# Layer 2 of a fused attention and two-layer MLP kernel: the second product from seven quarter products, in an order made by a list scheduler

## The chip, the cores and the metric

The kernel runs on one core of a Trainium2 chip. The metric is the device time of one execution in microseconds (us); the time before is the median of 3 runs. Engines: PE is TensorE's matmul stream and PEld its weight loads, DVE is VectorE, ACT is ScalarE, POOL is GpSimd, SP is SyncE, which issues most DMAs.

## The reference, cut to what matters

```python
attn = softmax(block_mask(q @ k.T / 8)) @ v     # 4 x 8 heads, 576 rows, 64 wide
x = attn.transpose(0, 2, 1, 3).reshape(2304, 512)
h = x @ w_in1;  g = where(h >= 1, h, where(h <= -1, 0, (h + 1) ** 2 / 4));  x = g @ w_out1
h = x @ w_in2;  g = h * cos(h);  out = g @ w_out2     # w_in 512 x 2048, w_out 2048 x 512
```

The change is in layer 2, the last line: `h = x @ w_in2`, `h * cos(h)`, and the product with `w_out2`.

## The kernel before, in words

All products on PE keep 32-bit accuracy by halves: an operand is split into a rounded part (hi) and the rest (lo), and each product is three matmuls, hi·hi, hi·lo, lo·hi. ACT makes the hi part, DVE the lo part (the helper `rest`, line 194).

Attention comes first, then layer 1 in five blocks of rows (four of 512 rows, and in the middle one of 256 rows, whose matmuls are therefore 256 columns wide), then layer 2 in `second()`. While layer 1 runs, `w_combine` fetches `w_in2` and `w_out2` in eight groups each, makes their parts on ACT, DVE and POOL, and stores them to DRAM: `w_in2` as seven combinations of its quarters, `w_out2` as it is.

Layer 2 takes the 2304 rows in three batches of 768. Each batch has two phases.

- First product (`first_product`, matmuls on line 900). Rows of x, features of x and columns of h are halved, so each of x, `w_in2` and h has four quarters, 11, 12, 21, 22. Seven products of sums of quarters (Strassen's scheme in Winograd's form) give all four quarters of h, where the plain product takes eight. A run is one of seven products (order `ROUND` = 1, 6, 2, 7, 5, 4, 3) for one of four column groups q: 12 matmuls of 384 columns. There are 28 runs. After a run, ACT copies its result out of PSUM or DVE adds it to a stored quarter. Run 3 goes on in the PSUM bank of run 5, two runs earlier, so its first matmul waits until DVE has read what run 5 left there. A tile of PSUM is two banks wide and there are four.
- `chain`: for each of 16 tiles of h, ACT makes the integer part of h/(2 pi) + 1/4, DVE takes it off in two steps (two constants, `C1` and `C2`), ACT takes the sine, DVE multiplies by h.
- Second product (`second_product`, line 985). It is the plain product: for each of 16 tiles, `pair` makes hi and lo, then two runs of 9 matmuls each, 512 columns wide, the tile as the weights and `w_out2` as the moving operand. 288 matmuls a batch, all into three PSUM tiles that are copied out at the end.

The weights come through a ring of ten buffers of 512 KB, fetched by SP up to nine ahead (`w2_fetch`, line 806). The next batch's x is loaded (`x2_load`, line 811) and split into seven operands (`x2_split`) in the second phase.

Engines run their instructions in program order. The order within `second()` comes from a clock of runs: `at(d, f)` puts f behind the run d steps later, and `chain` and `pair` start at most one tile each per run. `pin` (`keep_in_program_order`) fixes it.

Of the kernel before, what the change touches and what calls it, by code (L numbers as in the profile page):

```python
# [24 lines left out]
C1 = 6.28125  # L25
C2 = 2.0 * math.pi - C1

FLOOR = -0.5 + 2.0 ** -14


@with_exitstack
def attn_moe_moe_kernel(ctx: ExitStack, tc: tile.TileContext, q, k, v, w_in1, w_out1, w_in2, w_out2, out):
# [53 lines left out]
    wdi = [dram.tile([7, 128, 2, 512], F32, name=f"w2i{q}") for q in range(4)]  # L86
    wdo = [dram.tile([2, 128, 1024], F32, name=f"w2o{g}") for g in range(8)]
# [190 lines left out]
    def w_combine(g, which):  # L278
# [4 lines left out]
        plain = [M.F1.view((16 + 4 * i) * KB, [2, 512], F32R) for i in range(2)]  # L283
# [4 lines left out]

        def half_of(i):
            return v[:, 2 * i:2 * i + 2].rearrange("p a b -> p (a b)")  # L290

        def join(i):
            joined(half_of(i).bitcast(U32), raws[i])

        def hi(t, x):
            nc.scalar.activation(out=t, in_=x, func=ACTF.Copy)

        def lo(t, x, h):
            rest(t, x, h, nc.gpsimd)

        def split(d, t, x):
            if len(t.shape) == 4:
                h, l = t[:, :, 0], t[:, :, 1]
            else:
                h, l = t[:, 0], t[:, 1]
            at(d, lambda: hi(h, x))
            at(d + 1, lambda: lo(l, x, h))

        def combine():
            nc.vector.tensor_tensor(out=v[:, 3], in0=v[:, 2], in1=v[:, 3], op=ALU.add)  # L310
            sub(2, 0, 2)
            sub(0, 3, 0)
            sub(1, 1, 0)

        def store(i, n, t):
            dst = wdi[g // 2][i:i + n, :, g % 2].rearrange("i p x -> p i x")
            nc.gpsimd.dma_start(out=dst, in_=t.rearrange("p i a b -> p i (a b)").bitcast(F32))

        def store_plain(i):
            nc.gpsimd.dma_start(out=wdo[g][i], in_=plain[i].rearrange("p a b -> p (a b)").bitcast(F32))  # L320
# [5 lines left out]
        for i in range(2):  # L326
            at(1 + i, lambda i=i: join(i))
        at(3, free)
        if which == 1:
            for i in range(2):  # L330
                split(3 + i, plain[i], half_of(i))
                at(6 + i, lambda i=i: store_plain(i))
            return
        split(3, few[:, 0:2], v[:, 0:2])
        split(4, few[:, 2:3], v[:, 3:4])
        at(6, combine)
        for n in range(2):
            split(7 + n, many[:, 2 * n:2 * n + 2], v[:, 2 * n:2 * n + 2])
# [431 lines left out]
    HT = 384  # L770
    AT = {1: 0, 2: 1, 4: 2, 6: 3, 3: 4, 7: 5, 5: 6}
    ROUND = (1, 6, 2, 7, 5, 4, 3)
    NR = 10
# [4 lines left out]
    def l2_views():  # L778
        L2.runs, L2.loads, L2.slot = [], [], {}
        for b in range(NBK):  # L780
            for q in range(4):
                for i in ROUND:
                    L2.slot["a", b, q, i] = len(L2.loads)
                    L2.loads.append((wdi[q][AT[i]], (2, 512)))
                    L2.runs.append(("a", b, q, i))
            for q in range(4):
                for i in (2, 1):
                    for e in range(2):
                        for j in (1, 2):
                            L2.slot["b", b, q, 10 * i + j, e] = len(L2.loads)  # L790
                            L2.runs.append(("b", b, q, 10 * i + j, e))
                        L2.loads.append((wdo[2 * q + e][i - 1], None))
# [3 lines left out]
        L2.wo = [(42 + 4 * n) * KB for n in range(NR)]  # L796
# [3 lines left out]
    def w2_fetch(upto):  # L800
        while L2.fetched < min(upto, len(L2.loads)):
            src, dims = L2.loads[L2.fetched]
            t = M.A1.view(L2.wo[L2.fetched % NR], [1024], F32R).bitcast(F32)
            if dims:
                src = src.rearrange("p e n -> p (e n)")
            nc.sync.dma_start(out=t, in_=src)
            L2.fetched += 1
# [9 lines left out]
    def x2_split(pin=lambda i: i):  # L817

        X = {(r, c): L2.x[:, 2 * r:2 * r + 2, HT * c:HT * (c + 1)] for r in range(2) for c in range(2)}
        hi = lambda i, x: pin(nc.scalar.activation(out=L2.xq[i][:, :, 0], in_=x, func=ACTF.Copy))  # L820
        lo = lambda i, x: pin(rest(L2.xq[i][:, :, 1], x, L2.xq[i][:, :, 0]))
        sub = lambda o, a, b: pin(nc.vector.tensor_tensor(out=X[o], in0=X[a], in1=X[b], op=ALU.subtract))
        c11, c12, c21, c22 = (0, 0), (0, 1), (1, 0), (1, 1)

        def split(i, c):
            return [lambda: hi(i, X[c]), lambda: lo(i, X[c])]

        return (
            split(1, c11) + [lambda: sub(c11, c12, c11)] + split(3, c22) + [lambda: sub(c12, c22, c12)]
            + [lambda: sub(c22, c22, c11)] + split(6, c22) + split(2, c21) + [lambda: sub(c21, c22, c21)]  # L830
            + split(7, c12) + split(5, c11) + split(4, c21)
        )
# [18 lines left out]
    def l2_late():  # L851
# [10 lines left out]
        L2.u = Slots(M.F1, 6 * KB, 3 * KB, 2)  # L862
# [10 lines left out]
    def second():  # L873
# [18 lines left out]
        def first_product(run):  # L892
# [13 lines left out]
            if i in (1, 5):  # L906
                held[i] = at_, ps
# [269 lines left out]
```

## Time and profile before

| what | value |
|---|---|
| median of 3 runs | 972.42 us (972.08 to 972.62) |
| the profiled execution's own time | 972.27 us |
| its span, first to last instruction | 970.1 us |
| outside the span | 2.17 us |
| busy: PE, DVE, ACT, POOL | 955.4, 645.6, 495.0, 332.9 us |
| granted clock, share of full speed | 0.997 |

Busy times of one engine are the union of its instructions in time. For PE that says little about its pace, since matmuls overlap; the pace is read as time from one start to the next.

### The profile page before, as it was taken

How to read it: one execution, taken by the hardware profiler on the slowest of the kernel's cores; microseconds unless marked ns; L12 is line 12 of the kernel's file. 1: busy time of each engine (PE TensorE's matmuls, PEld its weight loads, DVE VectorE, ACT ScalarE, POOL GpSimd, SP SyncE). 2: the span in 40 equal slices, each digit the busy share in tenths (PEclk: the TensorE clock that was granted, in tenths of full speed). 3: DMA queues.
4: the chain of work that ended last, by engine and by line, in shares of the span. 5: the costliest groups of instructions: out<-in, count | busy, mean ns of one | idle time of the engine just before them, and what ended most of it. 6: DMA issues, size and time to landing. Idle time of an engine off the chain costs nothing.

```text
span 970.1 us, 15896 instructions
## 1 busy us (share of the span) xinstructions
PE 955.4 (98%) x5876; PEld 823.4 (85%) x5876; DVE 645.6 (67%) x1022; ACT 495.0 (51%) x1001; POOL 332.9 (34%) x421
## 2 busy tenths in 40 slices
PE   8999999999999999999999999999999999999997
PEld 7777888778888889988888889998889988899886
DVE  5778888777766686763647423688917889277870
ACT  5778888874454545453535222346513465134550
POOL 3567767766756574744552110000000000000000
PEclk9999999999999999999999999999999999999999
DMA  5755556345266557543352434883388744587411
GB/s 118 204 138 154 145 146 162 100 147 173 87 206 218 178 180 250 195 156 138 118 195 100 163 120 134 254 258 129 124 295 259 251 140 130 203 270 252 149 39 66
DMA packets 122509, 163.57 MB, mean 169 GB/s; under 512 B 62784, under 2 KB 91456, under 8 KB 122432
## 3 DMA queue, kind: packets, MB, share of 16 engines
q1 hardware_dynamic: 116288, 139.49, 46.2%
q0 software_dynamic: 6144, 23.07, 6.2%
q8 instruction: 47, 0.77, 0.4%
q14 instruction: 30, 0.25, 0.1%
HBM read 125.30 MB, written 37.22 MB: 168 GB/s over the span
## 4 chain that ended last, share of the span: by engine, by line
PE 79%; DVE 8%; ACT 8%; issue 2%; POOL 1%; DMA 1%; SPq 1%; ACTq 0%; DVEq 0%; POOLq 0%
PE q L985 20%; PE a L747 19%; PE h L701 19%; PE q L900 18%; ACT P L490 7%; DVE m L479 2%; DVE f L227 1%; DVE d L508 1%; DVE f L223 1%; DVE PT L560 1%; POOL m L194 1%; DMA rk<-in_k_dram 1%; PE s L451 1%; PE s L546 1%; PE s L577 1%
## 5 line engine op out<-in xcount | busy, mean ns | idle before, releaser
L985 PE MATMUL q<-m 128*128 128x512 f32 x864 | 196.4, 389 | 0.0
L985 PEld LDWEIGHTS q<-m 128*128 128x128 f32 x864 | 162.2, 188 | 33.5
L900 PE MATMUL q<-m 128*128 128x384 f32 x1008 | 175.3, 334 | 0.0
L900 PEld LDWEIGHTS q<-m 128*128 128x128 f32 x1008 | 174.9, 188 | 0.2
L747 PE MATMUL a<-g,m 128*128 128x512 f32 (+1 forms) x780 | 172.0, 368 | 0.4 <-DVE g L194 0.4
L747 PEld LDWEIGHTS a<-g,m 128*128 128x128 f32 x780 | 137.0, 189 | 25.1 <-DVE g L194 0.8
L194 DVE TENSOR_TENSOR g<-f,g 128x512 fp32r<-128x512 f32 (+1 forms) x80 | 78.4, 981 | 67.2 <-POOL g L191 66.9
L718 ACT ACTIVATE f<-h,half 128x512 f32<-128x512 f32 (+1 forms) x80 | 51.4, 642 | 132.6 <-PE h L701 120.3
L191 POOL TENSOR_SCALAR g<-f 128x512 fp32r<-128x512 f32 (+1 forms) x80 | 56.4, 704 | 162.6 <-DVE f L724 153.1
L519 POOL TENSOR_SCALAR P<-P,r 128x576 f32<-128x576 f32 (+2 forms) x144 | 91.2, 650 | 50.7 <-DVE r L511 31.3
L890 ACT ACTIVATE f<-f,hpi 128x768 f32<-128x768 f32 x48 | 45.1, 940 | 116.7 <-DVE f L887 116.6
L490 ACT ACTIVATE P<-s,m 128x288 f32<-128x288 f32 (+4 forms) x160 | 81.3, 523 | 36.3 <-DVE m L485 28.4
L701 PE MATMUL h<-m 128*128 128x512 f32 (+1 forms) x468 | 98.9, 360 | 0.0
L701 PEld LDWEIGHTS h<-m 128*128 128x128 f32 x468 | 79.1, 192 | 13.2 <-issue 0.7
L724 DVE SCALAR_TENSOR_TENSOR f<-f,h 128x512 f32<-128x512 f32 (+1 forms) x80 | 50.2, 627 | 43.7 <-ACT f L721 43.5
L701 PE MATMUL h<-x,m 128*128 128x512 f32 x312 | 75.9, 389 | 0.0
L223 DVE SCALAR_TENSOR_TENSOR f<-f 128x512 uint32<-128x512 uint32 x64 | 44.8, 721 | 38.8 <-ACT f L216 30.2
L479 DVE TENSOR_REDUCE m<-s 128x1 f32<-128x288 f32 (+4 forms) x160 | 67.1, 472 | 2.7 <-PE s L451 2.6
L701 PEld LDWEIGHTS h<-x,m 128*128 128x128 f32 x312 | 58.3, 188 | 11.8
L451 PE MATMUL s<-K,Q 128*128 128x288 f32 (+4 forms) x320 | 66.3, 462 | 1.3 <-ACT P L490 1.2
L887 DVE SCALAR_TENSOR_TENSOR f<-f 128x768 f32<-128x768 int32 x60 | 57.4, 957 | 4.7 <-ACT f L890 2.9
L577 PEld LDWEIGHTS s<-PT,rv 128*64 128x64 f32 x960 | 45.4, 137 | 14.1 <-ACT PT L562 9.3
(109 smaller groups left out, 1361.8 us busy)
## 6 DMA issues: line engine op xcount, KB each, us to landing
m<-w2i SPq DMA_DIRECT2D x84, 512.0 KB, 4.3
m<-w2o SPq DMA_DIRECT2D x48, 512.0 KB, 3.5
f<-in_moe_w_in_dram SPq DMA_DIRECT2D x32, 512.0 KB, 4.5
f<-in_moe_w_out_dram SPq DMA_DIRECT2D x32, 512.0 KB, 3.8
w2i<-f POOLq DMA_DIRECT2D x8, 1024.0 KB, 5.6
w2o<-f POOLq DMA_DIRECT2D x16, 512.0 KB, 3.1
w2i<-o POOLq DMA_DIRECT2D x8, 768.0 KB, 4.1
rk<-in_k_dram SPq DMA_DIRECT2D x32, 144.0 KB, 3.0
```

The costliest lines, as they stand in the source:

```text
L191: return nc.gpsimd.tensor_scalar(out=hi, in0=raw, scalar1=1.0, scalar2=1.0, op0=ALU.mult, op1=ALU.mult)
L194: return (eng or nc.vector).tensor_tensor(out=lo, in0=raw, in1=hi.bitcast(F32), op=ALU.subtract)
L451: mm = lambda o, l, r, **kw: pin(nc.tensor.matmul(out=o, lhsT=l, rhs=r, skip_group_check=True, **kw))
L479: i = P.top = nc.vector.tensor_reduce(out=m[:, c:c + 1], in_=o, axis=AX.X, op=ALU.max, negate=True)
L490: P.act = nc.scalar.activation(out=pr[:, a:b], in_=o, func=ACTF.Exp, bias=m[:, e:e + 1], accum_out=den[:, c:c + 1],)
L519: P.div = nc.gpsimd.tensor_scalar(out=pr[:, a:b], in0=pr[:, a:b], scalar1=r[:, e:e + 1], scalar2=1.0, op0=ALU.mult, op1=ALU.mult,)
L577: pin(nc.tensor.matmul(out=ps[64 * h:64 * h + 64, c0:c0 + nq], lhsT=V[:, j, h, :], rhs=PT[:, a:a + nq], start=(j == 0), stop=(j == i), ski ...
L701: nc.tensor.matmul(out=hps[s][:, 0:n_], lhsT=w[:, a, kk * 128:(kk + 1) * 128], rhs=x[:, b], start=(kk == 0 and n == 0), stop=(kk == NK - 1 ...
L747: nc.tensor.matmul(out=o, lhsT=w[:, a, dm:dm + 128], rhs=b, start=(f == 0 and n == 0 and c == 0), stop=(f == NF - 1 and n == 2), skip_grou ...
L887: pin(nc.vector.scalar_tensor_tensor(out=o, in0=a, scalar=c, in1=b, op0=ALU.mult, op1=ALU.add))
L900: pin(nc.tensor.matmul(out=ps[:, e, 0:HT], lhsT=w[:, e, a, 128 * kk:128 * (kk + 1)], rhs=L2.xq[i][:, kk, c], start=(not src and kk == 0 an ...
L985: pin(nc.tensor.matmul(out=ps[:, s], lhsT=t[:, e, a, 128 * m:128 * (m + 1)], rhs=w[:, o], start=(q == 0 and c > 20 and e == 0 and n == 0), ...
```

## The change

- `w_combine` treats both weights alike: `w_out2` too is combined to seven operands and stored as `w2o` in the shape of `w2i` (`AT` gives the places). ACT scales `w_in2` by 1/(2 pi) on the way (`turns`), so h comes out in turns.
- `cosine` replaces `chain`: in turns, the integer part comes off in one DVE instruction; the multiplication by 2 pi is in the last one.
- `second_product` is the seven-product scheme. A run is 18 matmuls of 256 columns, for one of seven products i and one of four groups q, in the order `ORDER`. The operands of products 5, 6, 7, 3 are differences or sums of tiles of g, made by `operand_sum` (two tiles in one instruction of 1536 elements). The results go out one product at a time, by ACT copies and DVE additions of 768 elements.
- All operations of `second()` are given to `Plan` with an engine, a cost and the data they read and write. `Plan.run` emits them: PE's runs stay in the order given, those of DVE, ACT and SP are taken as they come ready in its own reckoning, the one with the longest path behind it first.

```diff
+class Plan:
+    def add(self, eng, cost, reads, writes, fn):
...
+    def run(self):
...
+            i = min((i for i in ready[e] if ready_at[i] <= t), key=lambda i: (-left[i], i))
+            ready[e].remove(i)
+            self.ops[i][3]()
...
-    wdo = [dram.tile([2, 128, 1024], F32, name=f"w2o{g}") for g in range(8)]
+    wd = [[dram.tile([7, 128, 2, 512], F32, name=f"w2{'io'[which]}{q}") for q in range(4)] for which in range(2)]
...
+        def turns():
+            nc.scalar.activation(out=flat, in_=flat, func=ACTF.Copy, scale=INV2PI)
...
         def combine():
-            nc.vector.tensor_tensor(out=v[:, 3], in0=v[:, 2], in1=v[:, 3], op=ALU.add)
-            sub(2, 0, 2)
-            sub(0, 3, 0)
-            sub(1, 1, 0)
+            if which == 0:
+                nc.vector.tensor_tensor(out=v[:, 3], in0=v[:, 2], in1=v[:, 3], op=ALU.add)
+                sub(2, 0, 2)
+                sub(0, 3, 0)
+                sub(1, 1, 0)
+            else:
+                sub(0, 1, 0)
+                sub(1, 3, 1)
+                sub(3, 3, 0)
+                sub(2, 3, 2)
...
+    ORDER = [(q, i) for i in (1, 4) for q in range(3)] + [(3, 1), (3, 4)]
+    ORDER += [(q, i) for i in (2, 5, 6, 7, 3) for q in range(4)]
...
-            def s2():
-                stt(u, e, -C1, h)
-                stt(u, e, -C2, u)
...
+            act_(k, h, [G], [E], ACTF.Identity, bias=quarter)
+            tt(r, h, k, sub, [G, E], [E])
+            act_(r, r, [E], [E], ACTF.Sin, bias=hpi, scale=2.0 * math.pi)
+            do("V", 0.96, [E, G], [G], lambda: pin(nc.vector.scalar_tensor_tensor(
+                out=h, in0=h, scalar=2.0 * math.pi, in1=r, op0=ALU.mult, op1=ALU.mult
+            )))
...
+        FROM = {1: (11,), 2: (21,), 4: (22,), 5: (22, 12), 6: (22, 11), 7: (11, 12), 3: (21, 22)}
+        def operand_sum(i, q):
+            x, y = FROM[i]
+            tt(*(L2.g[o][:, 2 * q:2 * q + 4] for o in (x, x, y)), add if i == 5 else sub,
...
-            for m in range(3):
-                i, s = divmod(3 * j + m, 2)
...
-                for n, (a, o) in enumerate(((0, 0), (0, 1), (1, 0))):
-                    pin(nc.tensor.matmul(
-                        out=ps[:, s], lhsT=t[:, e, a, 128 * m:128 * (m + 1)], rhs=w[:, o],
...
+                for e in range(2):
+                    for m in range(3):
+                        for n, (a, o) in enumerate(((0, 0), (0, 1), (1, 0))):
+                            pin(nc.tensor.matmul(
+                                out=ps[:, m // 2, 256 * (m % 2):256 * (m % 2) + 256],
+                                lhsT=t[:, e, a, 128 * m:128 * (m + 1)], rhs=w[:, e, o],
...
+            do("P", 2.16, [T], [bk], emit)
...
+            if i in (1, 4, 5):
+                copy(i)
+            elif i == 2:
+                copy(0)
+                store(0, 0, 0)
+            elif i == 6:
+                plus(1, 1)
+            elif i == 7:
+                plus(0, 1)
+                tt(Y[4], Y[0], Y[4], sub, [("y", 0), ("y", 4)], [("y", 4)])
+                store(4, 1, 0)
+                tt(Y[5], Y[0], Y[5], add, [("y", 0), ("y", 5)], [("y", 5)])
+                store(5, 1, 1)
+            else:
+                plus(1, 1)
+                store(1, 0, 1)
```

Three places show what the order becomes. The first is PE at the start of the second product of the first batch, before the change (`q` with a number is a PSUM tile, `m` holds the operands):

```order
L985 MATMUL q_6711<-m 128x512 [waits DMAHW0_49,Activation_49]
L985 MATMUL q_6711<-m 128x512 x5
L985 MATMUL q_6718<-m 128x512 [waits PE_49]
L985 MATMUL q_6718<-m 128x512 x5
L985 MATMUL q_6729<-m 128x512 [waits DVE_49]
L985 MATMUL q_6729<-m 128x512 x5
```

Here two runs of 9 share one weight buffer and spread over three PSUM tiles. The same place on PE after the change:

```order
L1062 MATMUL q_6807<-m 128x256 [waits DMAHW0_49,Activation_49]
L1062 MATMUL q_6807<-m 128x256 x17
L1062 MATMUL q_6807<-m 128x256 [waits DMAHW1_49]
L1062 MATMUL q_6807<-m 128x256 x17
L1062 MATMUL q_6807<-m 128x256 [waits DMAHW2_49]
L1062 MATMUL q_6807<-m 128x256 x17
```

Each run of 18 now has a weight buffer and a pair of its own, stays in one PSUM tile, and its matmuls are half as wide.

The second place is DVE in the first batch's first product, column group q = 1, before the change. Rows of line 884 that read `q` are the additions after runs 7, 5, 4 and 3; line 887 takes the integer part off; the other row of 884 is the last step of a chain.

```order
L884 TENSOR_TENSOR g<-q_6411,w 128x768 [waits PE_49]
L884 TENSOR_TENSOR f<-q_6428,g 128x768 [waits DMASW3_49,DMASW4_49,DMASW2_49,DMASW5_49,DMASW1_49,DMASW6_49,DMASW0_49,DMASW7_49,DVE_49,PE_49]
L884 TENSOR_TENSOR g<-g,q_6444 128x768 [waits DVE_49,PE_49]
L884 TENSOR_TENSOR g<-g,f 128x768 [waits Activation_49]
L887 SCALAR_TENSOR_TENSOR f<-f,w 128x768 [waits Activation_49]
L887 SCALAR_TENSOR_TENSOR f<-f 128x768 [waits DVE_49]
L884 TENSOR_TENSOR w<-q_6428,w 128x768 [waits PE_49]
```

The additions after runs 7, 5 and 4 stand one behind the other. The same place on DVE after the change (988 has the additions, 935 takes the integer part off, 1025 is the last step of a chain, 251 makes a lo part):

```order
L988 TENSOR_TENSOR g<-q_6488,w 128x768 [waits DVE_49,PE_49]
L1025 SCALAR_TENSOR_TENSOR w<-w,f 128x768 [waits Activation_49]
L988 TENSOR_TENSOR f<-q_6506,g 128x768 [waits DMASW3_49,DMASW5_49,DMASW1_49,DMASW7_49,DVE_49,PE_49]
L935 TENSOR_TENSOR f<-w,f 128x768 [waits Activation_49]
L988 TENSOR_TENSOR g<-g,q_6524 128x768 [waits DVE_49,PE_49]
L935 TENSOR_TENSOR f<-f 128x768 [waits Activation_49]
L988 TENSOR_TENSOR w<-q_6506,w 128x768 [waits PE_49]
L1025 SCALAR_TENSOR_TENSOR w<-w,f 128x768 [waits Activation_49]
L1025 SCALAR_TENSOR_TENSOR f<-f 128x768 [waits Activation_49]
L251 TENSOR_TENSOR m<-f,m 128x2x384
```

A chain step that waits for ACT now stands between the additions after runs 7 and 5, another between those after 5 and 4, and a pair for the second product is made already here.

The third place is DVE late in the second product of the first batch, before the change (194 makes lo parts, of tiles `g`, `f`, `w` and of the next `x`; 822 is a difference of quarters of `x`).

```order
L822 TENSOR_TENSOR x<-x 128x2x384
L884 TENSOR_TENSOR g<-g,f 128x768
L194 TENSOR_TENSOR m<-g,m 128x2x384 [waits PE_49,Activation_49]
L194 TENSOR_TENSOR m<-x,m 128x2x384 [waits Activation_49]
L884 TENSOR_TENSOR w<-w,f 128x768
L194 TENSOR_TENSOR m<-f,m 128x2x384 [waits PE_49,Activation_49]
```

Chains still end here, between the lo parts. The same place on DVE after the change:

```order
L935 TENSOR_TENSOR f<-f,w 128x1536 [waits DVE_49]
L251 TENSOR_TENSOR m<-f,m 128x2x384 [waits PE_49,Activation_49]
L935 TENSOR_TENSOR w<-w 128x1536 [waits DVE_49]
L251 TENSOR_TENSOR m<-f,m 128x2x384 [waits PE_49,Activation_49]
L935 TENSOR_TENSOR f<-f,w 128x1536 [waits DVE_49]
L251 TENSOR_TENSOR m<-f,m 128x2x384 [waits PE_49,Activation_49]
```

The chains have moved ahead of this stretch, and operand sums of 1536 elements stand between the lo parts.

## Rows read from the trace of the kernel before

**Rows 1.** The page: busy us of each engine, share of the span, instructions.

```profile
PE 955.4 (98%) x5876; PEld 823.4 (85%) x5876; DVE 645.6 (67%) x1022; ACT 495.0 (51%) x1001; POOL 332.9 (34%) x421
```

**Rows 2.** The chain that ended last, layer 2: start us, us, what, matmuls.

```profile
594.09 58.26 PE q L900 x336
652.35 65.32 PE q L985 x288
717.67 58.26 PE q L900 x336
775.94 65.32 PE q L985 x288
841.26 58.26 PE q L900 x336
899.52 65.34 PE q L985 x288
```

**Rows 3.** The same chain in layer 1's block of 256 rows.

```profile
383.94 1.44 PE a L747 x12
385.38 1.44 PE h L701 x12
...
402.78 2.88 PE h L701 x24
```

**Rows 4.** Windows (us): busy of PE, PEld, DVE, ACT, POOL, granted clock, DMA share, GB/s.

```profile
380.00:400.00 20.00, 20.00 (x169) 20.00 (x169) 13.05 (x24) 10.85 (x23) 11.34 (x15) 1.00 0.52 187
400.00:500.00 100.00, 100.00 (x521) 86.17 (x520) 58.34 (x81) 45.32 (x80) 51.59 (x61) 1.00 0.40 143
```

**Rows 5.** Groups from 594 to 970 us, DVE.

```profile
L884 DVE TENSOR_TENSOR w<-w,f 128x768 f32<-128x768 f32 x24 | 22.8, 950 | 0.0
L884 DVE TENSOR_TENSOR f<-q,g 128x768 f32<-128x768 f32 x12 | 11.5, 958 | 1.2
L998 DVE COPY o<-q 128x1024 f32<-128x1024 f32 x3 | 3.7, 1225 | 44.9 <-PE q L985 44.9
```

**Rows 6.** Windows of layer 2's first four phases, columns as in rows 4.

```profile
593.90:652.20 58.30, 58.30 (x338) 58.27 (x337) 39.98 (x46) 24.15 (x29) 0.00 (x0) 1.00 0.82 257
652.20:717.60 65.40, 65.40 (x290) 54.15 (x290) 47.84 (x54) 30.39 (x37) 0.00 (x0) 1.00 0.48 161
717.60:776.00 58.40, 58.40 (x338) 58.37 (x337) 39.48 (x44) 23.52 (x28) 0.00 (x0) 1.00 0.81 270
776.00:841.00 65.00, 65.00 (x288) 53.82 (x287) 47.48 (x53) 30.39 (x37) 0.00 (x0) 1.00 0.42 137
```

**Rows 7.** Groups, ACT, from 594 to 970 us.

```profile
L890 ACT ACTIVATE m<-w 128x768 fp32r<-128x768 f32 x24 | 19.9, 830 | 0.5 <-DVE w L884 0.5
L890 ACT ACTIVATE o<-q 128x1024 f32<-128x1024 f32 x3 | 3.1, 1029 | 47.8 <-PE q L985 47.8
```

**Rows 8.** DMA issues from 594 to 970 us: KB each, median us to landing.

```profile
m<-w2i SPq DMA_DIRECT2D x74, 512.0 KB, 4.3
m<-w2o SPq DMA_DIRECT2D x48, 512.0 KB, 3.5
out_dram<-o SPq DMA_DIRECT2D x6, 512.0 KB, 2.8
x<-x2d SPq DMA_DIRECT2D x3, 512.0 KB, 6.3
out_dram<-x SPq DMA_DIRECT2D x3, 512.0 KB, 5.6
```

**Rows 9.** Line 900, its instructions: duration ns min/median/max, first and last start.

```profile
L900 PEldq EVENT_SEMAPHORE  x82: 51/51/51, 589.9 to 894.2; - x82
```

**Rows 10.** The timeline's end: start us, us, engine, line, what.

```profile
964.88 1.02 ACT L890 ACTIVATE x<-q 128x1024 f32<-128x1024 f32 x1 [1.69 <-PE q L985]
965.93 0.37 SPq L1002 DMA_DIRECT2D out_dram<-x  x1
```

**Rows 11.** Groups by line and shape, PE: busy us, mean ns of one, idle before.

```profile
L747 PE MATMUL a<-g,m 128*128 128x256 f32 x156 | 21.4, 283 | 0.0
```

More of the change, by code (lines that the diff above doesn't have):

```diff
@@ L778, in l2_views @@
     def l2_views():
-        L2.runs, L2.loads, L2.slot = [], [], {}
+        L2.runs = []
         for b in range(NBK):
[L781 to L792, printed above, removed]
+            L2.runs += [("a", b, q, i) for q in range(4) for i in ROUND]
+            L2.runs += [("b", b, q, i) for q, i in ORDER]
         M.X.renew(F32)
@@ L800, in w2_fetch @@
     def w2_fetch(upto):
[L801 to L806, printed above, removed]
+        while L2.fetched < min(upto, len(L2.runs)):
+            kind, b, q, i = L2.runs[L2.fetched]
+            which = "ab".index(kind)
+            nc.sync.dma_start(
+                out=L2.w[L2.fetched % NR].rearrange("p e a n -> p (e a n)").bitcast(F32),
+                in_=wd[which][q][AT[which][i]].rearrange("p e n -> p (e n)"),
+            )
             L2.fetched += 1
@@ new lines, in tt, with act_, taken @@
+        def tt(o, a, b, op, reads, writes, wide=1):
+            do("V", WIDE[wide], reads, writes, lambda: pin(nc.vector.tensor_tensor(out=o, in0=a, in1=b, op=op)))
+        def act_(o, a, reads, writes, func=ACTF.Copy, **kw):
+            do("A", 0.84 if func is ACTF.Copy else 0.93, reads, writes, lambda: pin(
+                nc.scalar.activation(out=o, in_=a, func=func, **kw)
+            ))
+        place = {r: n for n, r in enumerate(L2.runs)}
+        last, tiles = [-4, -3, -2, -1], {}
+        def taken(n):
+            at_ = min(range(4), key=lambda i: last[i])
+            tiles[at_, n] = None
+            last[at_] = 10 ** 9
+            return at_, n
@@ L1012, in second @@
[L1012 to L1025 removed]
+            key = held.pop(src) if src else taken(place[run])
@@ new lines, in first_product, with emit @@
+            bk = ("ps", key[0])
+            def emit():
+                w2_fetch(place[run] + NR - 1)
+                w, ps = L2.w[place[run] % NR], ps_of(key)
+                for e in range(2):
+                    for kk in range(2):
+                        for n, (a, c) in enumerate(((0, 0), (0, 1), (1, 0))):
+                            pin(nc.tensor.matmul(
+                                out=ps[:, e, 0:HT], lhsT=w[:, e, a, 128 * kk:128 * (kk + 1)], rhs=L2.xq[i][:, kk, c],
+                                start=(not src and kk == 0 and n == 0), stop=(kk == 1 and n == 2),
+                                skip_group_check=True,
+                            ))
@@ new lines, in second @@
+        next_x(1)
+        for b in range(NBK):
+            for run in L2.runs:
+                if run[1] != b or run[0] == "b":
+                    continue
+                first_product(run)
+                if run[2:] == (0, 1) and b + 1 < NBK:
+                    x_sums(b + 1)
+            if b + 1 < NBK:
+                x_splits(b + 1)
+            if b + 2 < NBK:
+                next_x(b + 2)
+            for q, i in ORDER:
+                if len(FROM[i]) == 2 and q % 2 == 0:
+                    operand_sum(i, q)
+                second_product(("b", b, q, i))
@@ L1028, in attn_moe_moe_kernel @@
+        plan.run()
     halves = [tuple(range(j, min(j + 2, NBLK))) for j in range(0, NBLK, 2)]
```

348 lines of the change are left out of this document (188 added, 160 removed).

## Prediction

> **What bounds the kernel now.** I read the page first: PE is busy 98% of the span, DVE 67%, ACT 51% [rows 1]. A busy PE need not be at its pace, so the second view is the chain that ended last. From 594.09 us to the last matmul it runs through PE alone, in six pieces: three first products of 58.26 us and three second products of 65.32 to 65.34 us [rows 2]. No other engine appears between them. The reader is to see that the 371 us of layer 2 are a count of matmuls times a pace: 58.26 us / 336 = 173.4 ns for 384 columns, 65.32 us / 288 = 226.8 ns for 512. So there are two questions: what the new matmuls take, and whether the other engines still keep up.
>
> **PE, the main term.** The second product is now 28 runs of 18 matmuls, 504 a batch and 1512 in all, in place of 864. They have 256 columns, and layer 1's block of 256 rows shows matmuls of that width, each with its own 128x128 weights, in the same order of parts (the same weights twice, then another): 12 in 1.44 us on either line, 24 in 2.88 us, so 120.0 ns [rows 3]. The window in the same stretch counts 169 in 20 us, 118 ns [rows 4]. I take 120.0.
>
> - Before: 65.32 + 65.32 + 65.34 = 195.98 us. After: 1512 x 0.120 = 181.44 us. Difference: **-14.5 us**.
> - The first products stay as they are: 3 x 58.26 us [rows 2].
>
> The Trainium skill prices this differently. Its page "TensorE: Matmul & The Clock Gate", section "Back-to-back issue gap", has a spacing of columns / 2.4 plus 2.5 ns, so 109.2 ns at 256 columns; by it the second product would take 165.1 us and the sum would be 941.8 us. The trace does not agree: it is 11 ns above that formula at 512 columns (226.8 against 215.8) and 11 ns at 256.
>
> **DVE.** A batch has, by the order, 20 additions after runs of the first product (as before), 32 chain steps where there were 48, 28 lo parts where there were 16, 5 additions on the way out where there was 1 copy, 11 operations for the next x (as before), and 8 operand sums of 1536 elements. That is 104 instructions where there were 96. One of 768 elements takes 0.95 us [rows 5], but they overlap at their ends: 46 fill 39.98 us, so 0.87 us of DVE's time each [rows 6]. A sum of 1536 elements has no row. It must lie between 1.225 us (1024 elements) and twice 0.950 us; by the slope between 950 and 1225 ns it is 0.95 + 768 x 0.275 / 256 = 1.78 us [rows 5], less the 0.08 us overlap 1.70 us. A batch then needs 96 x 0.87 + 8 x 1.70 = 97 us, and PE gives it 58.26 + 60.48 = 118.7 us: 82%, where it was 39.98 + 47.84 = 87.8 us of 123.6 [rows 6].
>
> The tightest stretch is the first batch's first product: from the first addition to the last the order has 57 DVE instructions, 49.6 us, and the additions can begin only two runs (4.2 us) after the phase does, so 54 us are left for them. Such a place costs nothing while PE's next run hides it. What can show is run 3: it goes on in the bank of run 5, with only run 4, 12 x 0.1734 = 2.08 us, between. The addition after run 5 takes 0.96 us [rows 5], so one DVE instruction (0.95 us) still fits ahead of it and two lose 0.96 + 2 x 0.95 - 2.08 = 0.78 us. The order has one ahead of it, a chain step that waits for ACT's sine. There are 12 such places: from 0 to 9.4 us. Before, this wait existed too, and PE idled 0.0 us in all of layer 2's chain [rows 2]; I stay near that row and take **+0.4 us**, half an instruction in all. Queued behind a late chain step on DVE are the addition, then run 3 on PE, and PE's order is fixed, so all that follows would move.
>
> **ACT.** A batch has 79 instructions. At 0.83 us for a copy of 768 elements, and less than the 1.03 us of 1024 for any other [rows 7], they take 66 to 81 us of 118.7; ACT matters as the one that the chain steps wait for.
>
> **Weights and SP.** Every run of the second product now fetches 512 KB: 28 a batch where there were 16. With the next x (1.57 MB) and the output (1.57 MB) a second product moves 14.7 + 3.1 = 17.8 MB in 60.5 us, 294 GB/s. First products moved 257 and 270 GB/s at a DMA share of 0.82 and 0.81 [rows 6]; by that ratio 294 GB/s is a share of 0.9. A fetch lands 3.5 to 4.3 us after issue, an x load 6.3 us [rows 8], and SP fetches nine runs ahead, 9 x 2.16 = 19 us. SP's queue holds the x loads and stores among the fetches, each waiting for DVE; 19 us covers such a wait. Cost 0; without that cover, see the rivals.
>
> **Waits on PE's queue.** A run that waits for more than one engine carries an extra semaphore instruction of 51 ns; the first products have 82 such and keep 173.4 ns [rows 2, 9]. At 120 ns there is less room beside it: from 0 to 84 x 0.051 = 4.3 us. I take 0, by the nearest row.
>
> **Layer 1.** Each of the eight groups of `w_out2` gets four DVE differences, two more hi and lo parts and larger stores, each group of `w_in2` an ACT scaling of 1024 elements, 1.03 us [rows 7]. In the stretch where `w_out2` is treated PE is busy 100.00 of 100 us while POOL is busy 51.59, DVE 58.34, ACT 45.32; and groups of `w_in2`, with about this work, passed while PE was busy 20.00 of 20 us [rows 4]. Cost 0; were ACT's part exposed, 8 x 1.03 = 8.2 us.
>
> **The end.** Before, ACT reads the last PSUM tile for 1.02 us, and the last store is issued at 965.93 us, 4.2 us before the span ends [rows 10]. Now DVE adds for 0.96 us and the store is 393 KB in pieces of 1 KB. By landing times of 2.8 to 6.3 us [rows 8] this is -1.4 to +2.1 us. I take 0.
>
> **Sum:** 972.27 (the profiled execution's own time, 0.15 us under the median) - 14.5 + 0.4 = **958.2 us**.
>
> **The rivals.**
>
> - *DVE late at run 3* (between 961 and 968 us). Two instructions ahead at all 12 places give 957.8 + 9.4 = 967.2 us, at half of them 962.5 us. For it: a step waiting for ACT stands at that place now, and the first stretch has DVE at nine tenths. Against: the 32 chain steps end early enough that the sum over a batch leaves DVE 22 us.
> - *DMA bounds the second product* (963 to 969 us). If 270 GB/s, the most that a phase showed, were all there is, 17.8 MB take 65.9 us, 5.4 us over, in the two batches that have a next x: 968.6 us. Against: the share was 0.81 then [rows 6].
> - *Slower: the weight loads bind at 256 columns.* The group of such matmuls is busy 21.4 us for 156, 137 ns each [rows 11], and in that stretch the weight loads are busy 20.00 of 20.00 us [rows 4], so any stumble of theirs shows. At 137 ns the 1512 take 207.1 us: 983.4 us. It decides from 195.98 / 1512 = 129.6 ns. Against: the chain's 120.0 ns, which spans whole pieces [rows 3]; the 21.4 us include overlapping ends. In the second product the weight loads were busy 54.15 of 65.4 us, 83% [rows 6]. The Trainium skill, "Perfetto Trace Analysis", section "Identifying the Most-Contended Engine", says to judge PE by the weight loads' busy share and not the matmuls'; by that rule the change takes the second product to its limit, which speaks against it, but the page names no loss.
> - *No gain.* Pairs made just in time: each run's third matmul waits for the lo part from DVE. 14.5 us / 84 runs = 0.17 us a run is enough to end at 972 us. Against: six pair buffers let DVE be six runs ahead.
> - *Faster: the fixed part of a matmul goes away.* From 384 to 512 columns the pace grows by 53.4 ns, 0.417 ns a column [rows 2], so 256 columns alone are 106.8 ns and some 13 ns a matmul are fixed. Were these hidden in the second product, it would take 1512 x 0.1068 = 161.5 us: 938.2 us. Against: 120.0 ns [rows 3] is 106.8 plus the same 13. The Trainium skill's spacing, above, points this way.
>
> **How the numbers follow.** My forecast 0.68 (956.5 to 961 us), DVE late 0.18, DMA 0.06, weight loads 0.04, no gain 0.03, no fixed part 0.01. The predicted time is that of the first. The range goes from 956 us (the end's gain of 1.4 us and no stall give 956.4) to 966 us, which takes in most of the second and a part of the third case, some 0.84. A measurement of this kernel tells about 0.2% (2 us) from no change. Faster: 0.68 + 0.18 + 0.06 + 0.01 = 0.93; same 0.03; slower 0.04.
>
> **What would show it.** In the chain, layer 2 is six pieces again, three of 58.3 us with 336 matmuls of 384 columns, three of 60.5 us with 504 of 256. PE's idle time before its groups stays under 1 us. DVE is busy about 82% of layer 2 and waits mostly for ACT. A time over 961 us should show PE waiting for DVE at runs 3 of the first product (line 970); DMA as the bound would show PE waiting for `w2o` fetches on line 1062; a pace over 125 ns on line 1062 without any wait would make the main term wrong.

## The result, and the profile after

The changed kernel takes 959.25 us (median of 4 runs, 958.83 to 959.64); the kernel before took 972.25 us beside it (971.69 to 972.62). The ratio is 0.9867, 95% interval 0.985 to 0.9884. 958.2 us were predicted. The profiled execution took 959.37 us, its span is 957.5 us (970.1 before) and the mean granted clock is 0.996.

The page of the changed kernel, busy us of each engine, beside [rows 1]:

```profile
PE 943.0 (98%) x6524; PEld 843.4 (88%) x6524; DVE 703.3 (73%) x1078; ACT 542.2 (57%) x1067; POOL 349.2 (36%) x437
```

PE is still busy 98%, with 648 more matmuls. As before, this row says nothing about the pace; the chain does. The chain that ended last, layer 2 of the changed kernel (start us, us, what, matmuls), beside [rows 2]:

```profile
596.48 58.26 PE q L970 x336
654.75 60.47 PE q L1062 x504
715.22 58.24 PE q L970 x336
773.46 60.47 PE q L1062 x504
833.93 58.24 PE q L970 x336
892.17 60.48 PE q L1062 x504
952.65 0.02 issue
952.67 0.96 DVE o L1089
```

The reader is to see three things. The six pieces are of PE alone, as before. A second product takes 60.47 us where it took 65.32 us, and 60.47 us / 504 = 120.0 ns a matmul. And layer 2 begins at 596.48 us, 2.39 us later than before, which no step of the prediction had.

The account, from the two profiled executions: layer 2 to its last matmul 356.17 us for 370.77 us (-14.6); its start +2.4; from the last matmul to the end of the span 4.85 us for 5.24 us (-0.4); outside the span 1.87 us for 2.17 us (-0.3). The sum is -12.9 us, which is 959.37 - 972.27.

Windows of the changed kernel's first four phases (columns as in [rows 4]), beside [rows 6]:

```profile
596.40:654.70 58.30, 58.30 (x338) 58.30 (x337) 49.66 (x56) 38.81 (x47) 0.00 (x0) 1.00 0.76 259
654.70:715.20 60.50, 60.50 (x506) 60.50 (x505) 51.59 (x52) 27.87 (x35) 0.00 (x0) 1.00 0.79 269
715.20:773.40 58.20, 58.20 (x338) 58.20 (x337) 48.43 (x54) 36.33 (x44) 0.00 (x0) 1.00 0.80 280
773.40:833.90 60.50, 60.50 (x506) 60.50 (x505) 48.63 (x49) 28.71 (x36) 0.00 (x0) 1.00 0.76 258
```

DVE (third number) has gone from 39.98 to 49.66 us in the first product and from 47.84 to 51.59 us in the second; over layer 2's six phases it is busy 288.38 of 356.2 us, 81%. The weight loads (second) are now busy in every microsecond of the second product. The DMA share is 0.76 to 0.80 and PE waits for no fetch. The granted clock is 1.00.

In layer 2 PE's waits are empty. In layer 1 there is this one, of the waits of PE (us in total, times, longest):

```profile
PE a L801 <- DVE g L251: 1.3, 3, 0.8
```

1.0 us of it falls between 400 and 500 us. The window there, beside the last of [rows 4]:

```profile
400.00:500.00 100.00, 99.03 (x515) 84.73 (x514) 77.14 (x104) 49.47 (x90) 66.00 (x73) 1.00 0.53 189
```

PE was busy 100.00 us here and is now busy 99.03 us; DVE went from 58.34 to 77.14 us and POOL from 51.59 to 66.00. In this stretch `w_out2` gets its parts.

### The profile page after: what moved, and what is told of

It reads as the page before. It is cut to its first block, busy times and chain, and to the rows that moved or that the text cites. A ratio compares the mean times of both kernels' runs of the same rounds, so it can differ in the third digit from the quotient of the medians.

```text
span 957.5 us, 17583 instructions
## 1 busy us (share of the span) xinstructions
PE 943.0 (98%) x6524; PEld 843.4 (88%) x6524; DVE 703.3 (73%) x1078; ACT 542.2 (57%) x1067; POOL 349.2 (36%) x437
## 4 chain that ended last, share of the span: by engine, by line
PE 76%; DVE 10%; ACT 8%; issue 2%; POOL 2%; DMA 1%; SPq 0%; ACTq 0%; DVEq 0%; POOLq 0%
PE q L1062 19%; PE a L801 18%; PE q L970 18%; PE h L755 18%; ACT P L544 7%; DVE m L533 2%; DVE f L284 1%; DVE d L562 1%; DVE f L280 1%; DVE PT L614 1%; POOL m L251 1%; DVE g L251 1%; PE s L505 1%; DVE f L343 1%; PE h L166 1%
## 5 line engine op out<-in xcount | busy, mean ns | idle before, releaser
L1062 PE MATMUL q<-m 128*128 128x256 f32 x1512 | 181.9, 283 | 0.0
L1062 PEld LDWEIGHTS q<-m 128*128 128x128 f32 x1512 | 181.8, 192 | 0.0
L970 PEld LDWEIGHTS q<-m 128*128 128x128 f32 x1008 | 174.7, 188 | 0.1
L251 DVE TENSOR_TENSOR g<-f,g 128x512 fp32r<-128x512 f32 (+1 forms) x80 | 70.8, 885 | 54.8 <-POOL g L248 54.7
L631 PE MATMUL s<-PT,rv 128*64 128x128 f32 (+1 forms) x960 | 52.4, 260 | 2.3 <-ACT PT L616 2.3
```

Source lines behind the costliest of these rows:

```text
L251: return (eng or nc.vector).tensor_tensor(out=lo, in0=raw, in1=hi.bitcast(F32), op=ALU.subtract)
L631: pin(nc.tensor.matmul(out=ps[64 * h:64 * h + 64, c0:c0 + nq], lhsT=V[:, j, h, :], rhs=PT[:, a:a + nq], start=(j == 0), stop=(j == i), ski ...
L970: pin(nc.tensor.matmul(out=ps[:, e, 0:HT], lhsT=w[:, e, a, 128 * kk:128 * (kk + 1)], rhs=L2.xq[i][:, kk, c], start=(not src and kk == 0 an ...
L1062: pin(nc.tensor.matmul(out=ps[:, m // 2, 256 * (m % 2):256 * (m % 2) + 256], lhsT=t[:, e, a, 128 * m:128 * (m + 1)], rhs=w[:, e, o], start ...
```

## The experiments

Each run stands beside runs of the kernel before on the same chip; these took 972.45 us in the runs of layer 1 and of half width, 974.5 us in those of DVE, order and ring, and 972.99 us in the last four. Absolute times are compared within one of these groups, and otherwise ratios. The first three runs ask where the 2.4 us at the start of layer 2 come from.

**1. Without w_out2's differences.** This kernel leaves out the four differences of each group of `w_out2`. Parts and stores are issued as in the changed kernel, on data that isn't combined.

```diff
             else:
-                sub(0, 1, 0)
-                sub(1, 3, 1)
-                sub(3, 3, 0)
-                sub(2, 3, 2)
+                return
```

> The changed kernel, with the combination of w_out2 left out: its four DVE differences a group and what follows them (parts of the four combined operands and their store), so the output is not the reference's. In the changed kernel layer 2 starts at 596.48 us, 2.4 us later than before, 1.9 us of it lost between 415 and 430 us, where w_out2 is prepared beside layer 1. Theory (the added preparation holds the lo parts of layer 1's g on DVE): without it the loss goes, layer 2 starts at 594.1 to 595.1 us, PE's wait for DVE on line 801 falls from 1.3 us to under 0.5, and the time is 957.0 to 958.0 us. Rival (the loss is the chance of one execution, or comes from the larger stores of the first three operands, which stay): 596 to 597 us again and 959.2 us.

Measured: 957.45 us (956.99 to 957.9), ratio 0.9845, interval 0.983 to 0.986. The expectation speaks of what follows the differences as left out too; it was not, so this is the cost of the four differences alone. Window of this run:

```profile
400.00:500.00 100.00, 100.00 (x520) 86.16 (x520) 57.37 (x82) 48.64 (x89) 66.07 (x74) 1.00 0.55 194
```

PE is back at 100.00 of 100 us, with POOL as busy as in the changed kernel. So DVE's 32 differences cost PE time in layer 1. In the changed kernel the chain that ended last leaves PE there and runs through a difference (line 343) and a lo part of `g` (line 251):

```profile
408.53 2.09 DVE f L343
...
423.54 0.96 DVE g L251
424.49 1.44 DVE f L343
428.00 2.46 DVE g L251
```

In the kernel before and in this run, the same stretch of the chain is of PE alone.

**2. w_out2's lo parts on DVE in place of POOL.** This gives DVE more work and POOL less.

```diff
-            rest(t[:, :, 1], x, t[:, :, 0], nc.gpsimd)
+            rest(t[:, :, 1], x, t[:, :, 0], nc.gpsimd if which == 0 else nc.vector)
```

> The changed kernel, with the lo parts of w_out2 made on DVE and not on POOL. Theory A (stretching: DVE's two-tensor operations take 0.78 us where 0.42 us is their undisturbed time, while POOL makes lo parts beside them; POOL's work is what stretches them): w_out2's DVE differences of 256 elements fall from 775 ns to under 550 ns, the loss goes, layer 2 starts at 594.1 to 595.3 us, time 957.0 to 958.3 us. Theory B (queueing: what stands ahead of the lo parts of g on DVE is too much, however fast): DVE has 32 more instructions in this stretch, the loss grows, layer 2 starts at 597 us or later, time 959.5 us or more.

Measured: 957.88 us (957.28 to 958.11), ratio 0.9849, interval 0.9834 to 0.9863. Groups of DVE in 400 to 530 us (busy us, mean ns of one, idle before), of the changed kernel:

```profile
L343 DVE TENSOR_TENSOR f<-f 128x256 f32<-128x256 f32 x32 | 24.8, 775 | 3.5 <-POOL o L251 3.2
L251 DVE TENSOR_TENSOR g<-f,g 128x512 fp32r<-128x512 f32 x20 | 21.7, 1087 | 15.4 <-POOL g L248 15.4
L778 DVE SCALAR_TENSOR_TENSOR f<-f,h 128x512 f32<-128x512 f32 x20 | 13.6, 681 | 2.4 <-ACT f L775 2.4
```

and of this run:

```profile
L251 DVE TENSOR_TENSOR g<-f,g 128x512 fp32r<-128x512 f32 x20 | 14.9, 747 | 4.8 <-POOL g L248 4.8
L343 DVE TENSOR_TENSOR f<-f 128x256 f32<-128x256 f32 x32 | 14.8, 462 | 0.0
L251 DVE TENSOR_TENSOR f<-f 128x512 fp32r<-128x512 f32 x16 | 14.5, 908 | 0.5
L778 DVE SCALAR_TENSOR_TENSOR f<-f,h 128x512 f32<-128x512 f32 x21 | 14.3, 681 | 3.6 <-ACT f L775 3.5
```

The same 32 differences take 462 ns each where they took 775, and the lo parts of `g`, for which PE waits, 747 ns where they took 1087. In 400 to 500 us DVE has 131 instructions for 104, and yet is busy 78.80 us for 77.14. POOL's lo parts, running beside them, had stretched DVE's subtractions. The stretching itself is not new: in the kernel before, POOL's lo parts of `w_out2` ran beside layer 1 too, and the lo parts of `g` took nearly as long, as they still do in run 1 (its row is the second):

```profile
L194 DVE TENSOR_TENSOR g<-f,g 128x512 fp32r<-128x512 f32 x21 | 20.7, 986 | 22.2 <-POOL g L191 22.1
L251 DVE TENSOR_TENSOR g<-f,g 128x512 fp32r<-128x512 f32 x20 | 18.7, 934 | 33.9 <-POOL g L248 33.9
```

PE lost nothing in either. The starts and durations in the changed kernel's trace show which of POOL's work matters. Of DVE's 28 subtractions of 512 elements on line 251 between 400 and 530 us, the 12 with nothing of POOL beside them took 677 to 695 ns, the 5 beside POOL's roundings alone 880 to 1120 ns, and the 11 beside its subtractions 692 to 2445 ns. Run 2 leaves the roundings on POOL, so 747 ns is still above the undisturbed time.

**3. The four differences on POOL.**

```diff
-        sub = lambda o, a, b: nc.vector.tensor_tensor(out=v[:, o], in0=v[:, a], in1=v[:, b], op=ALU.subtract)
+        eng = nc.gpsimd if which == 1 else nc.vector
+        sub = lambda o, a, b: eng.tensor_tensor(out=v[:, o], in0=v[:, a], in1=v[:, b], op=ALU.subtract)
```

> The changed kernel, with the four differences of each group of w_out2 on POOL and not on DVE. Theory B (queueing on DVE): DVE's queue is as before the change, the loss goes, layer 2 starts at 594.1 to 595.3 us, 957.0 to 958.3 us. Theory A (stretching by POOL's work): POOL gets 32 more two-tensor operations of about 0.75 us, so its rounding of g comes later and DVE's lo parts of g are stretched as much or more: layer 2 starts at 596.5 us or later, 959.3 to 963 us.

Measured: 958.39 us (956.96 to 958.79), ratio 0.9852, interval 0.9837 to 0.9867. The lo parts of `g` on DVE stay long, and those of 256 elements have become longer (925 ns in the changed kernel):

```profile
L251 DVE TENSOR_TENSOR g<-f,g 128x512 fp32r<-128x512 f32 x20 | 21.7, 1085 | 39.8 <-POOL g L248 39.8
L251 DVE TENSOR_TENSOR g<-f,g 128x256 fp32r<-128x256 f32 x8 | 10.4, 1306 | 2.9 <-POOL g L248 2.9
```

The whole time lies between the ranges of the two theories. DVE has fewer instructions here, and PE still waits for it, once, for 0.5 us. Long lo parts with a short queue cost nothing in run 1, and a long queue of short subtractions cost nothing in run 2. So both matter: how much stands in DVE's queue, and how long each subtraction takes beside POOL's work.

Whole times of these runs differ by little more than their intervals. One stretch can be read more closely: from the 480th matmul of layer 1's first product (line 755, 701 before) to layer 2's first matmul, worked out from the starts in each trace. What lies ahead of it, attention above all, is not in it: over all the profiled executions the stretch begins anywhere between 390.4 and 392.9 us.

| kernel | us | gaps between PE's starts of more than 0.26 us |
|---|---|---|
| before | 202.95 | none |
| changed | 204.83 | 0.47, 0.29, 1.15, 0.34 us, from 407 to 431 us |
| changed, once more (below) | 204.83 | 0.47, 0.28, 1.14, 0.34 us, the same places |
| 1, no differences | 202.95 | none |
| 2, lo parts on DVE | 203.06 | none |
| 2, once more (below) | 203.01 | none |
| 3, differences on POOL | 203.74 | 0.82 us, at 412 us |

So of the 2.4 us, 1.9 us are the change's; the other 0.5 us stand ahead of the stretch and are within its varying start. The loss repeats: runs 5 to 10, whose layer 1 is the changed kernel's, have 204.37 to 204.82 us, so it is 1.4 to 1.9 us, and run 4, with the layer 1 of before, has 202.95 us. Of the 1.9 us the four gaps hold 1.3 us over the pace of 0.227 us; the rest is spread too thin to name. The gaps stand beside the first two of the eight groups of `w_out2`, whose differences begin at 405 and 424 us, in or just behind the block of 256 rows, which PE leaves at 426 us. The six later groups, with the same work, show no gap. What sets the first two apart was not tested.

**4. The kernel before at half width.** Each matmul of the plain second product is made as two of 256 columns. It tells the change of width from the change of scheme.

```diff
-                for n, (a, o) in enumerate(((0, 0), (0, 1), (1, 0))):
-                    pin(nc.tensor.matmul(
-                        out=ps[:, s], lhsT=t[:, e, a, 128 * m:128 * (m + 1)], rhs=w[:, o],
+                for x in range(2):
+                    for n, (a, o) in enumerate(((0, 0), (0, 1), (1, 0))):
+                        pin(nc.tensor.matmul(
+                            out=ps[:, s, 256 * x:256 * (x + 1)], lhsT=t[:, e, a, 128 * m:128 * (m + 1)],
+                            rhs=w[:, o, 256 * x:256 * (x + 1)],
```

> The kernel before, with each matmul of the second product cut into two of 256 columns: the same columns, twice the matmuls (1728). Theory (a matmul takes 13.2 ns plus 0.417 ns a column, whatever its width here, and weight loads at every matmul add nothing): the second product takes 1728 x 0.120 = 207.4 us, 11.4 us more, 983.7 us in all; the chain shows 576 matmuls in 69.1 us. Rival (at 256 columns the weight loads are the limit only in long streams, or the first trace's 137 ns busy a matmul was the truth): 1728 x 0.137 = 236.7 us, 1013 us. Rival (no fixed part): 972 us.

Measured: 984.99 us (984.51 to 985.48), ratio 1.013, interval 1.0113 to 1.0147. Its chain:

```profile
653.37 69.11 PE q L986 x576
...
780.73 69.11 PE q L986 x576
908.08 69.12 PE q L986 x576
```

69.11 us / 576 = 120.0 ns again, whatever the scheme. The three pieces are 11.4 us longer than in [rows 2], and another 1.0 us of the 12.5 us is the later start of layer 2, 595.11 us. The change's gain is thus two effects: an eighth less of multiplication, 24.5 us of 195.98, less 10 us for narrower matmuls, since 120.0 ns is 6.6 ns more than half of 226.8 and 1512 x 6.6 ns = 10 us.

**5. A third DVE step in every chain.** An operation that changes nothing (the maximum of a tensor with itself), 16 a batch.

```diff
             tt(r, h, k, sub, [G, E], [E])
+            tt(r, r, r, ALU.max, [E], [E])
```

> The changed kernel with a third DVE step in each chain, as before the change (a maximum of the remainder with itself, in place of the second constant): 48 more DVE instructions of 0.87 us, 42 us, so DVE is busy about 94% of layer 2 in place of 82%. Theory (DVE's slack is real and the order is made anew around the extra step, so PE waits at a few runs 3 only): 0 to 3 us more, 959.2 to 962.5 us. Rival (at 94% an engine whose steps alternate with ACT's cannot keep up): PE waits 5 us or more for DVE in layer 2, 964 to 980 us.

Measured: 986.91 us (982.32 to 988.23), ratio 1.0113, interval 1.0086 to 1.0139; span 980.4 us. My theory fell. The rival's waits of 5 us or more came, and the time lies above its range too. PE's waits of the profiled execution, the fastest of the four:

```profile
PE q L1063 <- ACT m L939: 14.6, 3, 6.1
PE q L1063 <- DVE m L251: 2.4, 3, 1.2
```

All stand at one place, between the 108th and the 112th matmul of each second product. 108 / 18 is six runs, so it is the seventh, (q = 3, i = 1): the first that needs the last tile of quarter 11, whose chain ends late. Windows of PE around it in the second batch (busy of PE, granted clock, DMA share, GB/s):

```profile
778.00:786.00 8.00, 8.00 (x68) 1.00 0.85 263
786.00:794.00 8.00, 5.24 (x44) 0.99 0.77 253
794.00:802.00 8.00, 3.71 (x15) 0.50 0.02 6
802.00:810.00 8.00, 8.00 (x62) 0.87 0.54 181
810.00:818.00 8.00, 8.00 (x69) 1.00 0.76 235
```

A wait costs twice: PE idles, and in the window in which it begins again the granted clock is 0.50, the level of 1.2 GHz; it is back at 1.00 in the last window. 48 steps of 0.87 us are 42 us of DVE's time; layer 2 with the end (594.96 to 980.4 us) became 24.4 us longer than in the changed kernel, 17.0 us of it these waits.

**6. Without the list scheduler's order.** The operations are emitted as they are listed.

```diff
+        for op in self.ops:
+            op[3]()
+        return
```

> The changed kernel without the list scheduler's order: all operations of layer 2 are emitted as they are listed, each chain right behind its addition, each pair right ahead of its run, the seven splits of the next x ahead of the second product. DVE then waits for ACT twice in every chain with the next addition behind it: 4 chains of 2 x 0.95 + 2 x 0.93 us and 5 additions of 0.95 us a column group are 20 us where PE needs 14.6, so 21 us a first product, and some 6 us at the start of two second products. Theory: 1020 to 1045 us. Rival (in-order queues and six pair buffers even it out, so the order matters little): under 970 us.

Measured: 1191.51 us (1190.78 to 1193.22), ratio 1.2222, interval 1.2204 to 1.224; far over what I expected. PE's waits and a window of the first batch:

```profile
PE q L1065 <- ACT m L942: 90.3, 21, 16.1
PE q L973 <- ACT f L988: 61.2, 9, 6.8
PE q L1065 <- DVE m L254: 10.0, 21, 1.3
```

```profile
597.00:700.00 103.00, 65.76 (x327) 0.80 0.47 150
```

The scheme is the same, and in these rows PE waits 161.5 us, for pairs (`m`) and for copies of PSUM by ACT (line 988 of this run's kernel). The mean granted clock of the span is 0.919. On this chip the changed kernel would take 0.9867 x 974.5 = 961.5 us, by estimate, so the order is worth 230 us against this listing. It says nothing of the kernel before, which had an order of its own, from its clock of runs.

**7. The addition after run 5 three times**, in the first product. It tests the rival on run 3 by force.

```diff
-                out_(22, add, 21)
+                for _ in range(3):
+                    out_(22, add, 21)
```

> The changed kernel with the addition after each run 5 done three times (the same result each time), so that the last of them ends late; the order has one or two other DVE instructions among them. Theory (run 3 must wait for it and only run 4, 2.08 us, hides it): 4 or 5 instructions of 0.87 to 0.95 us are 3.5 to 4.6 us, 1.4 to 2.5 us of PE idle at each of 12 places, 17 to 30 us: 976 to 989 us, with PE waiting for DVE on line 970. Rival (PE is ahead of need there and DVE's slack of a fifth takes it): under 963 us.

Measured: 999.41 us (998.87 to 999.95), ratio 1.0249, interval 1.0229 to 1.027. PE's waits:

```profile
PE q L970 <- DVE f L988: 28.6, 12, 3.3
```

12 waits at the 12 places that the prediction named, 28.6 us, within what the expectation had for waits. The time is above the expectation. A window of PE behind the third wait of the first batch and the piece of the chain there show why:

```profile
640.00:650.00 10.00, 6.66 (x31) 0.84 0.48 148
```

```profile
645.47 16.44 PE q L970 x84
```

The granted clock is 0.84, and 16.44 us / 84 = 196 ns a matmul, where 173.4 ns is the pace at the full clock. I had priced the wait and not the clock behind it: from layer 2's first matmul to the end of the span this run takes 402.1 us for 361.0 us, 41.1 us more, of which the waits are 28.6 us.

**8. A ring of five buffers**, SP four fetches ahead and not nine.

```diff
-    NR = 10
+    NR = 5
```

> The changed kernel with five weight buffers in place of ten, so that fetches go four runs ahead (8.3 to 8.6 us) and not nine. Theory (a fetch lands 3.6 to 4.2 us after its issue and the DMA share of 0.8 leaves room): no loss in the steady run, 958.5 to 960.5 us. Rival (the DMAs are near their limit, and x loads and stores of 3.1 MB a batch need the deep ring as a store): PE waits for fetches on lines 970 and 1062 when x is loaded or results go out, 2 us or more: 961 to 970 us.

Measured: 961.57 us (960.17 to 965.92), ratio 0.9875, interval 0.9846 to 0.9904. The ratio can't be told from the changed kernel's. In the profiled execution (960.38 us) PE's starts show one gap in layer 2, of 0.39 us, and PE waits for no fetch there. That speaks against the rival with DMA as the bound: at half the lead nothing ran dry in it. Of the longest of the four executions, 965.92 us, there is no trace.

**9 and 10. The same 16 extra DVE steps, early or late.** Run 5 had them in all chains. Here they stand in half of the chains, two in each: in the column groups q = 0, 1 (early) or q = 2, 3 (late).

In the late one the condition is `q >= 2`.

```diff
+            for _ in range(2 if q < 2 else 0):
+                tt(r, r, r, ALU.max, [E], [E])
```

> The 16 extra DVE steps a batch of the three-step run, but all in the chains of the first two column groups (two extra steps in each of 8 chains), none in the last two. Theory (what counts is the backlog that DVE has when the first product ends: 57 instructions and 49.6 us of 54 as it is, and whatever extra work comes early is done in the idle time between the additions): PE waits in second products 0 to 6 us in all, time 959 to 967 us. Rival (it is the count alone, 73 instructions of 0.87 us = 63.5 us against 54, wherever they stand): PE waits for about the 17 us that the three-step run showed, time 982 to 990 us.

> The same 16 extra DVE steps a batch, all in the chains of the last two column groups (two extra in each of 8 chains). Theory (backlog at the end of the first product): at least the 17 us of PE waits of the three-step run and up to twice as much, again at the run of the second product that takes the last tile of quarter 11, time 983 to 1000 us. Rival (count alone): as the three-step run, 982 to 990 us, and the same as with the steps early.

Measured: early 974.96 us (973.56 to 975.53), ratio 1.0019, interval 1.0009 to 1.003; late 980.11 us (979.69 to 980.52), ratio 1.0072, interval 1.0052 to 1.0092. PE's waits in layer 2, early:

```profile
PE q L1064 <- DVE m L251: 5.1, 5, 1.3
PE q L970 <- DVE f L988: 3.2, 2, 2.3
PE q L1064 <- ACT m L939: 0.4, 1, 0.4
```

and late:

```profile
PE q L1064 <- DVE m L251: 7.4, 6, 1.2
PE q L1064 <- ACT m L939: 5.8, 4, 2.3
```

Two of the early run's waits, on line 970, are at a run 3 of the first product (q = 3). Neither theory gave these sizes. The rival, count alone, falls: 8.7 us early, 13.2 us late, 17.0 us spread evenly, for the same 48 instructions. Mine is right in sign only: early is the cheapest, but not free, and late is not the dearest. Layer 2 with the end grew by 14.5 us (early) and 19.3 us (late) in span. What is shown: in all three forms 14 us more DVE work a batch (42 us in all) is too much for DVE, and a fifth to two fifths of it come out as PE's waits. Which step pays is not settled: the scheduler reckons the added steps in and makes another order in each of these kernels, so the three differ in more than the place of the steps.

**11 and 12. The changed kernel and run 2 once more, on one chip.**

> The changed kernel itself, unaltered, on the same chip as the next run: 957.5 to 961 us, ratio 0.985 to 0.988.

> The changed kernel with the lo parts of the weights of the second product on DVE in place of POOL, once more, to be compared with the changed kernel on the same chip. If the 1.9 us lost in layer 1 come from DVE's differences being stretched beside POOL's lo parts: 1.0 to 2.0 us below the changed kernel of this call. Rival (the gap between 957.88 and 959.25 us was the difference of chips): within 0.5 us of it.

Measured: the changed kernel 960.46 us (959.76 to 962.09), ratio 0.9872, interval 0.9857 to 0.9887; with the lo parts on DVE 958.64 us (957.95 to 959.96), ratio 0.9852, interval 0.9835 to 0.9868. The difference of the medians is 1.8 us, within the 1.0 to 2.0 us expected, and that of the stretch in the table above 1.8 us; the two ratios' intervals overlap, so that it is faster rests on the stretch, which repeats in two profiles of each, more than on the whole times. With run 3, from which its time can't be told, it is the best complete version of these runs.

## Why the prediction was right, step by step

- **PE's pace at 256 columns, -14.5 us.** Right: 120.0 ns in the second product and in run 4, -14.6 us in the chain. That small pieces of another stage [rows 3] gave a price good to 0.1 ns over 1512 matmuls is the main reason that the forecast came out.
- **The fixed part of a matmul.** 106.8 + 13.2 ns held. The rival without it, and with it the Trainium skill's spacing ("TensorE: Matmul & The Clock Gate", section "Back-to-back issue gap"), would have ended at 938 to 942 us. That section of the Trainium skill calls the formula the "isolated single-MM gap"; for streams of weight loads and matmuls it has about 131 ns at 512 columns. The trace has 226.8 ns there, so neither figure fits these matmuls.
- **Weight loads.** The rival at 137 ns was wrong, though the group of such matmuls of before does read 137 ns [rows 11]: pieces of the chain are a pace, busy time over count is not (in the second product, with no short runs, it is 181.9 us / 1512 = 120.3 ns). The loads are busy 60.50 of 60.50 us and yet PE loses nothing: 120.0, 173.4 and 226.8 ns lie on one line, 53.4 ns for each 128 columns, while the loads' share is 100% at 256 columns and was 83% at 512. By the Trainium skill's rule to judge PE by the loads' share ("Perfetto Trace Analysis", section "Identifying the Most-Contended Engine") there would be no room left at 256 columns; the trace shows no loss from it, and no run tests whether a narrower matmul would show one.
- **DVE's load, 82%, and +0.4 us at run 3.** The load is 81%, an operand sum 1.752 us where 1.78 us was worked out, from this row of the group of sums:

```profile
L935 DVE TENSOR_TENSOR f<-f,w 128x1536 f32<-128x1536 f32 x12 | 21.0, 1752 | 0.0
```

  The stall was 0, not 0.4 us: PE waits nowhere in layer 2. The mechanism is real, as run 7 shows at exactly these 12 places, but in the changed kernel's order the step ahead of the addition isn't late: by the starts in the traces the addition ends 0.81 to 0.92 us ahead of run 3's first matmul at all 12 places, where it was 0.34 to 0.51 us in the kernel before. Against the prediction's 22 us a batch that DVE had left over, runs 5, 9 and 10 show that 14 us more do not fit. A likely reason, not shown by itself, is that the average of 81% hides the first product with 49.66 of 58.30 us.
- **DMA, 0.9.** Over-estimated: 0.79 at 269 GB/s in the window of the first second product. It cost nothing either way, as predicted, and run 8 shows how much lead was in hand.
- **Layer 1, 0.** This step failed, by +1.9 us. It took busy shares of 58% and 52% for room. What it missed is in the runs 1 to 3: in layer 1 PE waits for the lo part of `g` from DVE, the differences stand in that queue, and beside POOL's work DVE's subtractions take longer. Neither is a matter of share. Its other argument, that groups of `w_in2` pass without loss, held for them: from layer 1's first matmul on line 755 to the 480th, while ACT scales them, the changed kernel takes 199.4 us for 199.6 us. It didn't carry over to the first groups of `w_out2`.
- **The end, 0.** It was -0.4 us, within the -1.4 to +2.1 us. The last rows of the timeline of the changed kernel, beside [rows 10]:

```profile
952.67 0.96 DVE L1089 TENSOR_TENSOR o<-q,o 128x768 f32<-128x768 f32 x1 [5.82 <-PE q L1062]
953.66 0.37 SPq L1079 DMA_DIRECT2D out_dram<-o  x1
```

  The store is issued 3.8 us before the span's end, for 4.2 us before.

In sum the profiled execution ended 1.17 us above the forecast: +1.9 us of layer 1 and 0.5 us of a later start were missed, 0.4 us of stall did not come, and the end, the time outside the span and the main term were 0.8 us better. The main term was right by its mechanism; that the small errors nearly cancel is luck.

## What to carry to other kernels

Price a changed matmul by its pace at the new width, read over whole pieces of a chain elsewhere in the same trace, fixed part included; a scheme that saves an eighth of the multiplications by halving the width gave back 10 of 24 us here. Before an added instruction is costed at nothing, ask not how busy its engine is but who waits for what stands behind it in that engine's queue, and what runs on the other engines beside it. Where PE's order is fixed, a late operand can cost more than its wait: in runs 5 and 7 the granted clock behind the idle stretch was below 1.00 for a while.

## What was not expected of the hardware

DVE's subtractions of two tensors got longer while POOL worked beside them: with POOL's subtractions there 775 ns where 462 ns without for 256 elements, and 1087 for 747 ns for 512 (the changed kernel against run 2), one of them up to 2445 ns. POOL's roundings alone went with 880 to 1120 ns for 512 elements.

SCALAR_TENSOR_TENSOR on line 778 took 681 ns in both. It reads one of its two tensors, `h`, from PSUM, while the subtractions read both from SBUF. The kind of instruction is not what decides: in run 3 one SCALAR_TENSOR_TENSOR of line 280, which reads both from SBUF, took 1781 ns for a median of 686 ns, and POOL had begun a subtraction 0.09 us ahead of it. Others of its kind, on line 284, took 679 to 689 ns in the changed kernel, six of them beside a subtraction of POOL. Which inputs and which timing make an instruction long, these runs do not settle.
